# Linear-attention scan and two MLPs on one core: raw weights loaded into the tiles of their parts, prefix products spread by TensorE in the first block, a longer look ahead in the scheduler

## The chip, the core and the metric

The kernel runs on one core of a Trainium2 chip. The metric is the time of the core in microseconds (us), lower is better. The core has a matrix engine (PE), three other compute engines (DVE, ACT, POOL) that work from on-chip memory (SBUF; PE writes to PSUM, which DVE and ACT can read), and DMA queues. Here every transfer is issued by one queue, SP's, in the order of the program. Each engine executes its own instructions in the order written; across engines they wait for semaphores.

## What is computed

```python
def reference(x, a, B, C, moe_w_gate, moe_w_val, moe_w_out, moe_rms_g,
              moe2_w_in, moe2_w_out):          # weights arrive as float64
    # 1. scan over 24 chunks of 32 steps; batch 4, 8 heads, 768 steps, D 32, N 16
    la = log(clip(a, 1e-6, 1)); cum = cumsum(la, within the chunk)
    M  = (C B^T) * exp(cum_i - cum_j) * causal
    y  = M x + (C state) * exp(cum)
    state = exp(sum la) * state + sum_j B_j x_j exp(cum_end - cum_j)
    # 2. y becomes t[3072, 256]
    xn = t / sqrt(mean(t*t) + 1e-6) * moe_rms_g
    t  = (silu(xn @ w_gate) * (xn @ w_val)) @ w_out       # 256 -> 1536 -> 256
    # 3.
    h  = t @ w_in                                          # 256 -> 2048
    return (h * clip(h + 3, 0, 6) / 6) @ w_out2            # 2048 -> 256
```

## The kernel before

**Arithmetic.** A matmul in fp32 is done as three in fp32r: every operand is split into a high part (the value cast to fp32r) and a low part (the value minus the high part), and PE makes high·high, low·high and high·low (`mm3`, L642). Activations are split too: `xh`, `xl` are the parts of a block's input, `gh`, `gl` those of a hidden product.

**Weights.** They arrive as 8-byte floats and are turned into fp32 on the chip. For each tile f, `weights()` (L578 to L623) issues a load of the raw words (L585), then `low` and `high` on ACT (L598, L594), `join` and `sign` on DVE (L602, L607; integer operations on whole tiles), the high part as a cast on ACT or DVE (L245, L247) and the low part as a subtraction on DVE or POOL (L241, tiles `w1l`, `w2l`). There are 12 tiles of 128x768 for the first MLP (768 KB raw) and 16 of 128x512 for the second (512 KB raw). Raw tiles of the first go through a ring of six: three in the still unused result array `yT`, three (`rawx`) beside it. The intermediate fp32 tile has two places, also in `yT`. For the second MLP, `open2` frees the memory of the attention part and opens `w2h`, `w2l` and a ring of two raw tiles and two intermediate tiles (`cv`).

**Order of the work.** The 3072 rows fall into six blocks of 512. Each block needs four pieces of the scan (`attention(k)`, 24 in all), a norm, and then, in phase A, 12 steps: a step is 12 matmuls of 512 columns into `hps`, then on ACT a silu (L670), on DVE the product `p` (L678), `gh` on ACT (L685), `gl` on POOL or DVE (L241) and 6 matmuls into `acc`. The attention of the next block lies between the steps of a block. Phase B, the second MLP, has 16 steps per block (6 matmuls into `hps`, 6 into `acc`; L672 on ACT, L680 on DVE).

A piece k of attention: scores C·B on PE (L393); the decay matrix L as a scan on DVE (L366), which in the first block reads `aps`, a copy of the decays that PE spreads over the partitions (L358), and later a tile that a DMA spreads; the product SM on DVE (L402), two per piece; `bh` and `ch` on POOL or DVE (L241); the state step on PE (L411) and V on DVE (L422, L424); the result `y` on PE (L456, L462); its squares and transpose on ACT or DVE; the row mean on PE (L481) and `v` on DVE (L487). `ch` and V need P, the running products of the decays, spread over partitions: DVE makes them (`prefix`, L284), a DMA writes them to DRAM (`pref`, L298), and one DMA per piece reads them back spread (`ld_P`, L339). The norm ends with `rps` on PE (L532), the scaling on DVE (L538), `xh` on ACT and `xl` on DVE or POOL.

**The scheduler.** `Plan` holds all operations with estimated durations and dependences and simulates them: an engine that is free takes the ready operation with the longest tail (plus a boost). If an operation of much higher priority becomes ready within `WAIT` = 200 ns, the engine stays idle for it. Pieces of the first block have a boost of `BOOST0` = 15000. `either(n)` lets an operation go to DVE or POOL. In the first block's gaps PE multiplies zeros (`idle`, L305) as far as the first norm.

## Time and profile before

| | |
|---|---|
| runs, median (all) | 684.55 us (681.31, 684.55, 684.65) |
| profiled execution: its time, its span | 682.43 us, 680.3 us |
| PE busy | 659.6 us (97%) |
| DVE, ACT, POOL busy | 321.5, 292.3, 272.4 us |
| first matmul of the first MLP (first `hps`) | 39.69 us |
| norm of the second block (`rps`) | 99.20 us |
| norms of blocks three to six | 157.29, 219.35, 281.39, 342.53 us |
| last wait of PE that the trace shows | ends at 423.46 us |

All times of the trace count from the span's start. A block of phase A is the time from one `rps` to the next; phase B fills the time from 423.46 us to the end.

### The profile page before, as it was taken

What the parts mean: (1) busy time and instruction counts of PE and PEld (TensorE: products, weight loads), DVE (VectorE), ACT (ScalarE), POOL (GpSimd) and SP (SyncE); (2) the same over time, 40 slices, a digit from 0 to 9 for tenths busy, and PEclk for the clock granted to TensorE, in tenths of its full rate; (3) what the DMA queues carried; (4) which work ended last, traced back from release to release, by engine and by line L of the source; (5) the groups of instructions that cost most, each with busy time, mean ns of one, the idle gap of its engine ahead of it and who ended that gap; (6) DMA issues with size and microseconds to landing.
All of it is one profiled execution on the core that took longest, in us unless ns stands there. A gap on an engine that the chain in (4) does not pass through costs nothing.

```text
span 680.3 us, 10547 instructions
## 1 busy us (share of the span) xinstructions
PE 659.6 (97%) x4240; PEld 535.2 (79%) x4240; DVE 321.5 (47%) x532; ACT 292.3 (43%) x485; POOL 272.4 (40%) x223
## 2 busy tenths in 40 slices
PE   8879899999999999999999998999999999999997
PEld 7767677778778877877888876888888888888886
DVE  4798874554355345523268886232322322332222
ACT  2464442223222322332245666455444545454543
POOL 3334243233332342242234435454554545545443
PEclk9998899999999999999999999999999999999999
DMA  6965311130231031130003330000000000000000
GB/s 226 283 199 205 144 55 54 57 109 1 55 109 55 15 96 55 55 117 2 1 31 125 129 119 31 1 1 31 1 0 32 1 31 1 0 32 1 31 1 31
DMA packets 24464, 42.91 MB, mean 63 GB/s; under 512 B 2112, under 2 KB 15712, under 8 KB 24416
## 3 DMA queue, kind: packets, MB, share of 16 engines
q1 hardware_dynamic: 24416, 42.25, 19.0%
q8 instruction: 33, 0.54, 0.3%
q14 instruction: 15, 0.12, 0.1%
HBM read 38.90 MB, written 3.34 MB: 62 GB/s over the span
## 4 chain that ended last, share of the span: by engine, by line
PE 85%; DVE 9%; ACT 3%; issue 2%; DMA 0%; POOL 0%; SPq 0%; ACTq 0%; DVEq 0%; POOLq 0%
PE hps L642 46%; PE acc L642 30%; PE sps L462 2%; DVE p L678 2%; PE sps L456 1%; DVE SM L402 1%; PE sps L481 1%; ACT p L670 1%; DVE V L424 1%; DVE yT L607 1%; PE sps L393 1%; PE aps L358 1%; PE idle L305 1%; DVE yT L602 1%; PE rps L532 1%
## 5 line engine op out<-in xcount | busy, mean ns | idle before, releaser
L241 POOL TENSOR_TENSOR gl<-p,gh 128x512 fp32r<-128x512 f32 x158 | 209.1, 1324 | 267.0 <-ACT gh L685 254.4
L685 ACT CAST gh<-p 128x512 fp32r<-128x512 f32 x168 | 104.5, 622 | 126.7 <-PE acc L642 119.3
L680 DVE SCALAR_TENSOR_TENSOR p<-p,hps 128x512 f32<-128x512 f32 x96 | 65.9, 686 | 167.1 <-ACT p L672 167.0
L672 ACT ACTIVATE p<-hps,half 128x512 f32<-128x512 f32 x96 | 66.0, 687 | 79.3 <-POOL gl L241 77.6
L642 PE MATMUL hps<-xh,w1h 128*128 128x512 f32 x288 | 92.4, 402 | 0.1
L670 ACT ACTIVATE p<-hps 128x512 f32<-128x512 f32 x72 | 42.8, 595 | 113.4 <-PE hps L642 98.7
L678 DVE TENSOR_TENSOR p<-p,hps 128x512 f32<-128x512 f32 x72 | 49.2, 684 | 89.1 <-ACT p L670 88.3
L642 PE MATMUL hps<-xl,w1h 128*128 128x512 f32 x288 | 89.9, 393 | 0.5 <-DVE xl L241 0.4
L642 PE MATMUL hps<-xh,w1l 128*128 128x512 f32 x288 | 90.0, 394 | 0.0
L642 PE MATMUL acc<-gh,w2l 128*128 128x512 f32 x192 | 74.7, 389 | 0.0
L642 PE MATMUL acc<-gh,w2h 128*128 128x512 f32 x192 | 74.7, 389 | 0.0
L642 PE MATMUL acc<-gl,w2h 128*128 128x512 f32 x192 | 74.7, 389 | 0.0
L642 PEld LDWEIGHTS hps<-xl,w1h 128*128 128x128 f32 x288 | 54.6, 190 | 13.1 <-DVE xl L241 1.3
L642 PEld LDWEIGHTS hps<-xh,w1l 128*128 128x128 f32 x288 | 54.6, 190 | 11.9
L642 PE MATMUL hps<-xh,w2h 128*128 128x512 f32 x192 | 59.6, 392 | 2.5 <-DVE p L680 2.0
L642 PEld LDWEIGHTS hps<-xh,w1h 128*128 128x128 f32 x288 | 53.0, 191 | 10.5 <-ACT xh L245 0.6
L642 PE MATMUL acc<-gh,w1h 128*128 128x512 f32 x144 | 61.2, 425 | 0.0
L642 PE MATMUL hps<-xh,w2l 128*128 128x512 f32 x192 | 59.2, 389 | 0.0
L642 PE MATMUL hps<-xl,w2h 128*128 128x512 f32 x192 | 59.2, 389 | 0.0
L642 PE MATMUL acc<-gh,w1l 128*128 128x512 f32 x144 | 56.7, 394 | 0.0
L642 PE MATMUL acc<-gl,w1h 128*128 128x512 f32 x144 | 56.5, 393 | 0.0
L241 POOL TENSOR_TENSOR bh<-cb,L 128x256 f32<-128x256 f32 x22 | 14.6, 662 | 81.4 <-PE sps L411 64.5
(95 smaller groups left out, 836.9 us busy)
## 6 DMA issues: line engine op xcount, KB each, us to landing
cb<-comb SPq DMA_DIRECT2D x20, 576.0 KB
raw<-w SPq DMA_DIRECT2D x16, 512.0 KB
L<-azero SPq DMA_DIRECT2D x40, 128.0 KB
yT<-w SPq DMA_DIRECT2D x6, 768.0 KB
rawx<-w SPq DMA_DIRECT2D x6, 768.0 KB
out<-yT SPq DMA_DIRECT2D x12, 256.0 KB
P<-pref SPq DMA_DIRECT2D x24, 64.0 KB
cb<-comb SPq DMA_DIRECT2D x4, 320.0 KB
```

What stands on the lines that cost most here:

```text
L241: eng[e].tensor_tensor(out=out, in0=a, in1=b, op=op)
L305: pe.matmul(out=T["idle"][:, :128], lhsT=zero, rhs=zero, start=True, stop=True)
L358: pe.matmul(out=ps[64 * q:64 * q + 64, p * CH:(p + 1) * CH], rhs=az[:, q], lhsT=eye[:96, c:c + 1].to_broadcast([96, SC]), start=True, stop ...
L393: pe.matmul(out=bank2(ws[p // 2], "sps")[:, p % 2, c * SC:(c + 1) * SC], lhsT=cb[r, BN + c * 128:BN + (c + 1) * 128], rhs=cb[r, CT + c * S ...
L402: dve.tensor_tensor(out=T["SM", k][:, q], in0=T["w", ws[t]][:, :, 0:CH], op=ALU.mult, in1=T["L", k].rearrange("j (p c) i -> j p (c i)", c= ...
L462: pe.matmul(out=o[p][c], lhsT=cb[:, q:q + 64], rhs=SM[:, p, SC * c:SC * c + SC], start=False, stop=True, skip_group_check=True)
L642: pe.matmul(out=o, lhsT=a, rhs=c, start=first and i == 0, stop=last and i == len(seq) - 1)
L670: act.activation(out=p[:, :n], in_=T["w", hid][:, 0, :n], func=AF.Silu)
L672: act.activation(out=p[:, :n], in_=T["w", hid][:, 0, :n], func=AF.Relu, scale=1.0 / 6.0, bias=half)
L678: dve.tensor_tensor(out=p, in0=p, in1=h, op=ALU.mult)
L680: dve.scalar_tensor_tensor(out=p, in0=p, scalar=1.0, in1=h, op0=ALU.min, op1=ALU.mult)
L685: act.copy(out=t[:, :n], in_=T["p", i][:, :n])
```

## The change

There are three parts.

1. *Raw weights.* A raw tile is loaded into the memory in which its high and low part will stand later (`wt1`, `wt2`; a tile of twice the columns). Neither MLP has a ring of raw tiles any more. The high part overwrites the raw words once the intermediate tile is complete. The intermediate tile has eight places (instead of two) for the first MLP and four for the second.
2. *Prefix products.* In the first block (pieces 0 to 3) P comes from PE: POOL builds two selector tiles `rep` in the setup, `spread_p` multiplies them with `ac` (two matmuls of 128 columns), `copy_p` copies the result out of PSUM. The four DMAs of P that went with these pieces are gone. The later pieces read P by DMA as before.
3. *Scheduler.* An operation with a boost of at least `BOOST0` is waited for up to `FIRST` = 900 ns. The two DMAs to DRAM have a latency of 5000 ns in the plan. `prefix` has the highest priority.

```diff
-    WAIT, MARGIN = 200, 3000
+    WAIT, FIRST, MARGIN = 200, 900, 3000
...
-            soon = min((r for r, s in future[e] if r < t + self.WAIT and s not in done
+            soon = min((r for r, s in future[e] if s not in done
+                        and r < t + (self.FIRST if ops[s][4] >= BOOST0 else self.WAIT)
                         and -tail[s] - ops[s][4] < pri - self.MARGIN), default=None)
...
-    w1h = [cp.tile([128, 768], F32R, name=f"w1h{f}") for f in range(F1)]
-    w1l = [cp.tile([128, 768], F32R, name=f"w1l{f}") for f in range(F1)]
+    wt1, wt2 = {}, {}
+    wp1 = ctx.enter_context(tc.tile_pool(name="wp1", bufs=1))
+    for f in range(F1):
+        wt1[f] = wp1.tile([128, 1536], F32, tag=f"w{f}", name="raw")
...
+    rep = [ap1.tile([96, 4 * B, 2, N], F32, name=f"rep{q}") for q in range(2)]
...
-    rawx = [ap1.tile([128, 1536], F32, name=f"rawx{f}") for f in range(NRAW - 3)]
...
-              "sq": 1, "rn": 1, "x": 2, "p": 3, "gh": 3, "gl": 3, "raw": NRAW, "tmp": 2,
-              "raw2": 2, "cv": 2, "w": 3, "acc": 2})
+              "sq": 1, "rn": 1, "x": 2, "p": 3, "gh": 3, "gl": 3, "tmp": 8, "cv": 4, "w": 3, "acc": 2})
...
+        for q, t in enumerate(rep):
+            pool.memset(t, 0.0)
+            pool.affine_select(out=t[:, :, q], in_=t[:, :, q], pattern=[[1, 4 * B], [0, N]],
+                               compare_op=ALU.not_equal, fill=1.0, base=0, channel_multiplier=-1)
...
-             w=[("azero", 0)], boost=1e4)
-        P.op({"DVE": ds(256)}, prefix, r=[("az", 0)], w=[("ac", 0)], boost=1e4)
+             w=[("azero", 0)], boost=1e4, lat=5000)
+        P.op({"DVE": ds(256)}, prefix, r=[("az", 0)], w=[("ac", 0)], boost=1e9)
...
-        P.op(dma(65536), ld_P, r=[("pref", 0)], w=[("P", k)], boost=bst)
         if not first:
+            P.op(dma(65536), ld_P, r=[("pref", 0)], w=[("P", k)], boost=bst)
...
+        def spread_p(e):
+            for q in range(2):
+                pe.matmul(out=bank2(ws[0], "sps")[:, 0, 128:256], rhs=ac[:, q],
+                          lhsT=rep[q].rearrange("k a e n -> k (a e n)")[:, CH * k:CH * k + CH],
+                          start=q == 0, stop=q == 1, skip_group_check=True)
+
+        def copy_p(e):
+            T["P", k] = ap3.tile([128, CH], F32, tag="P", name="P")
+            copy(e, T["P", k], T["w", ws[0]][:, 0, 128:256])
...
         def load(e):
-            r = raw(f)
+            r = tiles[f][:, 0 if wide else cols:]
...
         def hi(e):
-            copy(e, wh[f], T[kt if wide else kr])
...
+            tiles[f] = pool().tile([128, 2, cols], F32R, tag=f"w{f}", name=f"w{tag}")
+            copy(e, tiles[f][:, 0], T[kt])
...
-        stage2.append(ctx.enter_context(tc.tile_pool(name="wp2", bufs=2)))
+        for f in range(F2):
+            wt2[f] = wp.tile([128, 1024], F32, tag=f"w{f}", name="raw2")
+        stage2.append(ctx.enter_context(tc.tile_pool(name="wp2", bufs=4)))
```

The lines of the changed kernel stand 1 to 26 higher: join and sign are L623 and L628, SM is L424, `v` is L508, the scan is L371, `two` is L242, the cast on DVE is L248, and the parts of a weight tile are both called `w`.

**DVE at the start, from the mean of piece 0 to the SM of piece 2.** Each row is an instruction of the queue with its output and inputs; `yT` in L602 and L607 is the intermediate weight tile. Before:

```order
L602 SCALAR_TENSOR_TENSOR yT<-yT 128x768
L487 TENSOR_SCALAR v_299<-sps 128x1
L607 SCALAR_TENSOR_TENSOR yT<-yT 128x768
L402 TENSOR_TENSOR SM<-sps,L 128x256 x2
L422 COPY V_324<-sps 128x64
L424 SCALAR_TENSOR_TENSOR V<-V_324,P,sps 128x64
L247 COPY xT<-sps 128x2x128
L241 TENSOR_TENSOR ch<-cb,P 128x64
L602 SCALAR_TENSOR_TENSOR yT<-yT 128x768
L487 TENSOR_SCALAR v_299<-sps 128x1
L607 SCALAR_TENSOR_TENSOR yT<-yT 128x768
L402 TENSOR_TENSOR SM<-sps,L 128x256 x2
```

After, from the scan of piece 2 to the last SM of piece 2:

```order
L371 SCALAR_TENSOR_TENSOR L<-aps,eye_107 128x512
L508 TENSOR_SCALAR v_272<-sps 128x1
L424 TENSOR_TENSOR SM<-sps,L 128x256 x2
L444 COPY V_299<-sps 128x64
L371 SCALAR_TENSOR_TENSOR L<-aps,eye_107 128x512
L508 TENSOR_SCALAR v_272<-sps 128x1
L424 TENSOR_TENSOR SM<-sps,L 128x256 x2
L444 COPY V_360<-sps 128x64
L446 SCALAR_TENSOR_TENSOR V<-V_299,P,sps 128x64
L446 SCALAR_TENSOR_TENSOR V<-V_360,P,sps 128x64
```

The joins and signs of the first two weight tiles, which stood ahead of the SM of pieces 1 and 2, are gone from here; only attention is left.

**DVE between the SM of piece 5 and that of piece 6** (`w1l`, `w` are weight parts, `p` the products of the steps, `ch` one of attention). Before:

```order
L424 SCALAR_TENSOR_TENSOR V1_711<-V_339,P_501,sps_676 128x64
L424 SCALAR_TENSOR_TENSOR V_715<-V1_711,P_501,sps_676 128x64
L241 TENSOR_TENSOR w1l6_92<-yT_73,w1h6_80 128x768
L241 TENSOR_TENSOR ch_744<-cb_631,P_671 128x128
L602 SCALAR_TENSOR_TENSOR yT_73<-yT_73 128x768
L607 SCALAR_TENSOR_TENSOR yT_73<-yT_73 128x768
L487 TENSOR_SCALAR v0_633<-sps_676 128x1
L247 CAST w1h7_81<-yT_73 128x768
L366 SCALAR_TENSOR_TENSOR L_746<-L_746,eye8_114 128x512
L602 SCALAR_TENSOR_TENSOR yT_73<-yT_73 128x768
L678 TENSOR_TENSOR p_776<-p_776,hps_756 128x512
L607 SCALAR_TENSOR_TENSOR yT_73<-yT_73 128x768
```

After:

```order
L628 SCALAR_TENSOR_TENSOR yT_73<-raw_82,yT_73 128x768
L623 SCALAR_TENSOR_TENSOR yT_73<-yT_73,raw_83 128x768
L248 COPY xT_585<-sps_650 128x2x128
L242 TENSOR_TENSOR ch_734<-cb_611,P_624 128x128
L628 SCALAR_TENSOR_TENSOR yT_73<-raw_83,yT_73 128x768
L248 CAST w_741<-yT_73 128x768
L508 TENSOR_SCALAR v0_602<-sps_650 128x1
L623 SCALAR_TENSOR_TENSOR yT_73<-yT_73,raw_84 128x768
L628 SCALAR_TENSOR_TENSOR yT_73<-raw_84,yT_73 128x768
L248 CAST w_765<-yT_73 128x768
L704 TENSOR_TENSOR p_762<-p_762,hps_743 128x512
L623 SCALAR_TENSOR_TENSOR yT_73<-yT_73,raw_85 128x768
```

More joins and signs stand here than before, and no low part. From the SM of piece 5 to that of piece 7 DVE has 13 joins and signs where it had 8, and no low part where it had 4; POOL has 5 to 7 low parts where it had one.

**POOL in the same stretch.** Before:

```order
L241 TENSOR_TENSOR gl_673<-p_648,gh_661 128x512
L241 TENSOR_TENSOR bh_708<-cb_631,L_616 128x256
L241 TENSOR_TENSOR gl_735<-p_669,gh_713 128x512
L241 TENSOR_TENSOR w1l7_93<-yT_73,w1h7_81 128x768
L241 TENSOR_TENSOR gl_800<-p_776,gh_796 128x512
L241 TENSOR_TENSOR bh_832<-cb_751,L_746 128x256
L241 TENSOR_TENSOR gl_859<-p_798,gh_837 128x512
```

After:

```order
L242 TENSOR_TENSOR gl_684<-p_645,gh_674 128x512
L242 TENSOR_TENSOR bh_701<-cb_611,L_592 128x256
L242 TENSOR_TENSOR w_722<-yT_73,w_722 128x768
L242 TENSOR_TENSOR w_741<-yT_73,w_741 128x768
L242 TENSOR_TENSOR w_765<-yT_73,w_765 128x768
L242 TENSOR_TENSOR gl_794<-p_762,gh_787 128x512
L242 TENSOR_TENSOR w_816<-yT_73,w_816 128x768
L242 TENSOR_TENSOR gl_858<-p_790,gh_827 128x512
L242 TENSOR_TENSOR w_860<-yT_73,w_860 128x768
```

Where single low parts stood between the `gl`, three now stand in a row (`w_722`, `w_741`, `w_765`, tiles 5 to 7), and two more alternate with `gl`.

**DVE at the end of phase A.** `raw_3818` to `raw_3911` of before and `raw_3339` to `raw_3341` of after are the last raw tiles of the second MLP; L680 and L706 are the products of phase B. Before:

```order
L602 SCALAR_TENSOR_TENSOR cv<-cv,raw_3818 128x512
L678 TENSOR_TENSOR p<-p,hps 128x512
L607 SCALAR_TENSOR_TENSOR cv<-raw_3818,cv 128x512
L680 SCALAR_TENSOR_TENSOR p<-p,hps 128x512
L602 SCALAR_TENSOR_TENSOR cv<-cv,raw_3865 128x512
L607 SCALAR_TENSOR_TENSOR cv<-raw_3865,cv 128x512
L680 SCALAR_TENSOR_TENSOR p<-p,hps 128x512
L241 TENSOR_TENSOR gl<-p,gh 128x512
L602 SCALAR_TENSOR_TENSOR cv<-cv,raw_3911 128x512
L680 SCALAR_TENSOR_TENSOR p<-p,hps 128x512
L607 SCALAR_TENSOR_TENSOR cv<-raw_3911,cv 128x512
L241 TENSOR_TENSOR gl<-p,gh 128x512
```

After:

```order
L623 SCALAR_TENSOR_TENSOR cv<-cv,raw_3339 128x512
L242 TENSOR_TENSOR w_3727<-cv,w_3727 128x512
L628 SCALAR_TENSOR_TENSOR cv<-raw_3339,cv 128x512
L704 TENSOR_TENSOR p<-p,hps 128x512
L623 SCALAR_TENSOR_TENSOR cv<-cv,raw_3340 128x512
L628 SCALAR_TENSOR_TENSOR cv<-raw_3340,cv 128x512
L242 TENSOR_TENSOR gl<-p,gh 128x512
L623 SCALAR_TENSOR_TENSOR cv<-cv,raw_3341 128x512
L704 TENSOR_TENSOR p<-p,hps 128x512
L628 SCALAR_TENSOR_TENSOR cv<-raw_3341,cv 128x512
L242 TENSOR_TENSOR gl<-p,gh 128x512
L704 TENSOR_TENSOR p<-p,hps 128x512 x2
```

Before, the last conversions lie between the products of phase B; now all of them lie ahead of the first one.

## Rows read from the trace of the kernel before

**Rows 1.** The page: busy time of PE over the span, and the shares of the chain that ended last, by engine.

```profile
PE 659.6 (97%) x4240; PEld 535.2 (79%) x4240; DVE 321.5 (47%) x532; ACT 292.3 (43%) x485; POOL 272.4 (40%) x223
...
PE 85%; DVE 9%; ACT 3%; issue 2%; DMA 0%; POOL 0%; SPq 0%; ACTq 0%; DVEq 0%; POOLq 0%
```

**Rows 2.** Windows of the span: start and end, length in us, then busy us (and instructions) of PE, of its weight loads, of DVE, ACT and POOL, the granted clock of PE as a share of full speed, the share of the DMA engines and GB/s. The first is from the first `hps` to the norm of block 2; the second lies inside it, from the SM of piece 5 to that of piece 7; then a whole block, the last block of phase A with the change of phase, and phase B.

```profile
39.60:99.10 59.50, 51.52 (x424) 39.82 (x424) 48.43 (x74) 30.59 (x48) 22.81 (x18) 0.91 0.42 148
59.97:88.25 28.28, 24.62 (x210) 18.92 (x208) 24.83 (x34) 15.13 (x24) 9.21 (x8) 0.94 0.43 150
157.20:219.20 62.00, 61.72 (x498) 49.25 (x497) 29.58 (x57) 18.49 (x35) 19.94 (x17) 1.00 0.19 60
342.40:423.40 81.00, 78.55 (x345) 63.35 (x343) 64.61 (x83) 48.63 (x86) 33.29 (x23) 1.00 0.26 91
423.40:676.00 252.60, 252.54 (x1114) 209.13 (x1115) 74.43 (x108) 125.69 (x196) 124.81 (x97) 1.00 0.03 11
```

**Rows 3.** The same view for the tile `hps` alone: the number behind PE's time is that of the 512-column matmuls.

```profile
39.60:99.10 59.50, 29.13 (x108) 21.59 (x108) 5.97 (x9) 5.37 (x9) 0.91 0.42 148
157.20:219.20 62.00, 34.33 (x144) 26.74 (x144) 8.19 (x13) 7.17 (x12) 1.00 0.19 60
342.40:423.40 81.00, 52.97 (x216) 40.08 (x216) 13.06 (x20) 12.08 (x20) 1.00 0.26 91
```

**Rows 4.** The same for the tile `acc`.

```profile
39.60:99.10 59.50, 12.27 (x42) 8.11 (x42) 0.00 (x0) 0.00 (x0) 0.91 0.42 148
157.20:219.20 62.00, 19.39 (x73) 12.82 (x72) 0.68 (x1) 0.58 (x1) 1.00 0.19 60
342.40:423.40 81.00, 30.46 (x121) 22.52 (x120) 0.68 (x1) 0.58 (x1) 1.00 0.26 91
```

**Rows 5.** The chain that ended last, in order of time: start, us, what.

```profile
157.29 0.89 PE rps L532 x8
158.18 5.48 PE hps L642 x24
...
219.35 0.89 PE rps L532 x8
...
342.53 0.89 PE rps L532 x8
```

**Rows 6.** Windows with a granted clock under full speed, columns as in rows 2.

```profile
48.40:54.90 6.50, 6.01 (x16) 4.94 (x17) 4.84 (x7) 1.24 (x3) 2.94 (x2) 0.51 0.96 333
75.20:78.70 3.50, 3.50 (x37) 2.88 (x38) 1.85 (x3) 0.65 (x2) 0.57 (x2) 0.51 0.48 141
```

**Rows 7.** DVE's timeline while the first four pieces run: start, us, line, operation, output and inputs, in brackets the idle time ahead.

```profile
10.96 1.22 DVE L366 TENSOR_TENSOR_SCAN L<-aps,eye 128x512 f32<-128x512 f32 x1 [1.50 <-PE aps L358]
...
14.76 0.28 DVE L424 SCALAR_TENSOR_TENSOR V<-V,P,sps 128x64 f32<-128x64 f32 x1
...
18.18 0.95 DVE L607 SCALAR_TENSOR_TENSOR yT<-yT 128x768 int32<-128x768 int32 x1
...
22.96 0.96 DVE L607 SCALAR_TENSOR_TENSOR yT<-yT 128x768 int32<-128x768 int32 x1
...
27.73 1.45 DVE L241 TENSOR_TENSOR bh<-cb,L 128x256 f32<-128x256 f32 x1
...
36.30 0.94 DVE L602 SCALAR_TENSOR_TENSOR yT<-yT,rawx 128x768 int32<-128x768 int32 x1
37.28 0.97 DVE L607 SCALAR_TENSOR_TENSOR yT<-rawx,yT 128x768 int32<-128x768 int32 x1
```

**Rows 8.** PE's timeline at the start: the last spreading of decays, the `y` step of piece 0, the mean of piece 3, the first matmul of the first MLP.

```profile
14.65 1.09 PE L358 MATMUL aps<-az,eye 96*64 96x128 f32 x16
15.68 0.34 PE L456 MATMUL sps<-ch,V 32*64 32x64 f32 x8
...
32.05 0.61 PE L481 MATMUL sps<-ones,sq 128*128 128x1 f32 x4 [0.65 <-ACT xT L245]
...
39.69 1.08 PE L642 MATMUL hps<-xh,w1h 128*128 128x512 f32 x2
```

**Rows 9.** DVE's timeline in the first block: casts, a scan, a low part and the SM of pieces 5 and 7.

```profile
51.58 0.56 DVE L247 CAST w1h<-yT 128x768 fp32r<-128x768 f32 x1
...
59.97 0.74 DVE L402 TENSOR_TENSOR SM<-sps,L 128x256 f32<-128x256 f32 x2
...
66.08 2.76 DVE L366 TENSOR_TENSOR_SCAN L<-L,eye 128x512 f32<-128x512 f32 x1 [0.24 <-DMA L<-azero]
...
71.19 1.54 DVE L247 CAST w1h<-yT 128x768 fp32r<-128x768 f32 x1
...
73.25 0.94 DVE L241 TENSOR_TENSOR w1l<-yT,w1h 128x768 fp32r<-128x768 f32 x1
...
88.25 0.74 DVE L402 TENSOR_TENSOR SM<-sps,L 128x256 f32<-128x256 f32 x2
```

**Rows 10.** POOL's timeline in the same stretch.

```profile
65.92 1.83 POOL L241 TENSOR_TENSOR w1l<-yT,w1h 128x768 fp32r<-128x768 f32 x1 [2.69 <-DVE w1h L247]
71.02 1.29 POOL L241 TENSOR_TENSOR gl<-p,gh 128x512 fp32r<-128x512 f32 x1 [3.26 <-ACT gh L685]
...
86.28 0.63 POOL L241 TENSOR_TENSOR bh<-cb,L 128x256 f32<-128x256 f32 x1 [0.30 <-PE sps L411]
```

**Rows 11.** PE's timeline at the first steps of phase B.

```profile
423.46 0.73 PE L642 MATMUL hps<-xh,w2h 128*128 128x512 f32 x2 [1.41 <-DVE p L680]
```

50 lines of the change are left out of this document (26 added, 24 removed).

## The prediction

> **What bounds the kernel now.** I read the page first. PE is busy for 97% of the span and holds 85% of the chain that ended last; DVE holds 9% of it, the DMA queues nothing [rows 1]. An average over the span hides where the rest is, so I cut the span at the norms. In a whole block of phase A PE works 61.72 of 62.00 us, in phase B 252.54 of 252.60 [rows 2]: there nothing but fewer matmuls could help, and the change removes none. What can move is the start (until the first `hps` at 39.69 us [rows 8]), the first block, and the change of phase, where PE misses 2.45 of 81.00 us [rows 2].
>
> How much each loses is a matter of counting matmuls. Twelve `hps` steps at full clock make 24 matmuls in 5.48 us, so one costs 0.228 us [rows 5]. A whole block lasts 219.35 − 157.29 = 62.06 us [rows 5] and holds 144 `hps` and 72 `acc` [rows 3, 4] (the window cuts one more `acc`): 49.2 us; 0.9 for `rps`; the other 12.0 are its attention. The first block until the norm of block 2 has 108 and 42 [rows 3, 4] and the same four pieces of attention: 150 × 0.228 + 12.0 = 46.2 us. It takes 59.5 [rows 2]. So 13.3 us are lost there. [...] DVE is busy for 48.43 of the 59.50 us [rows 2], and PE's attention steps wait for its SM and the steps for its `p`. In the change of phase 216 + 121 matmuls [rows 3, 4] and an `rps` make 77.7 us of 81.0; 3.3 are lost, 1.41 of them in the last wait for DVE's `p` [rows 11].
>
> **The start.** P of piece 0 no longer goes through two DMAs. V of piece 0 ran at 14.76, behind the scan of piece 2; now it stands behind the scan of piece 1, which began at 10.96 and took 1.22 [rows 7]. With `ch` and two small V steps between (about 0.7) the `y` step of piece 0 starts at about 13.3 instead of 15.68 [rows 8]: −2.3 us, and it passes the last spreading of decays, 1.09 us [rows 8], on the way. Then weight work leaves DVE's queue: an L607 of 0.95 ahead of the SM of piece 1, one of 0.96 ahead of that of piece 2, and a `bh` of 1.45 ahead of that of piece 3 that POOL now makes [rows 7]. Each was partly under PE's scores: I take 0.5, 0.8 and 0.9. The mean of piece 3 so comes at 32.05 − 4.5 = 27.6 [rows 8]. Behind it join and sign of one tile, 0.94 and 0.97 [rows 7], stood ahead of the scaling; now a join and a cast stand there: another −0.7. First `hps` at about 34.5: **−5.2 us** (bounds −3 and −6).
>
> The added work costs nothing here: two matmuls of 128 columns per piece and a copy on ACT stand where PE multiplied zeros and ACT waited; if the zeros did not cover them, four times about a third of a spreading of 1.09 us [rows 8] would be 1.5 us. The selector tiles are made while PE waits for its first data. The trace has no row for them; setting them aside at nothing is a choice, with 2.6 us as the upper bound, what two `gl` of POOL (1.29 each, of as many columns) take [rows 10].
>
> **The first block.** The start is earlier because the weights are later. Before, four of twelve tiles had been joined when the first `hps` began; now one is, and the other eleven are converted beside the steps. From the SM of piece 5 to that of piece 7 (28.28 us; DVE busy for 24.83, POOL 9.21 [rows 2]) DVE gets five joins or signs more (5 × 0.95 [rows 7]) and a `gl` (about 0.7, two thirds of a low part's 0.94), and gives four low parts to POOL (4 × 0.94 [rows 9]): +1.7 us for DVE by itself. POOL loses a `gl` (1.29) and gets four to six low parts of 1.83 [rows 10]: +6.0 to +9.7.
>
> On paper POOL has room for that. The trace says that the two don't run side by side. A cast on DVE took 0.56 alone, and 1.54 when it began at 71.19 beside a `gl` on POOL (71.02, 1.29 long); a scan took 1.22 alone [rows 7], and 2.76 when it began at 66.08 beside a low part on POOL that ended at 67.75 [rows 9, 10]. In both DVE's instruction ends where POOL's end plus its own time lie: 72.87 and 68.97 reckoned, 72.73 and 68.84 seen. SM and `p`, with an input in PSUM, aren't held up. So I add both engines' work on SBUF in one row: before, 8 joins and signs 7.6, 3 casts 1.7, 4 low parts 3.8, 2 scans 2.4 and a `ch` 0.3 on DVE; 4 `gl` 5.2, a low part 1.8, 2 `bh` 1.3 and a `ch` of about 0.5 on POOL: 24.6 of the 28.3 us. After: 24.6 + 1.7 + 6.0 to 9.7 = 32.3 to 36.0 us, and with the 3.7 that were free before, 36 to 40.
>
> [...]
>
> The SM of piece 5 comes some 3.6 us earlier than 59.97, at about 56.4 (the start's 5.2, less 1.6 for the join and low parts that now lie ahead of it); the SM of piece 7 then at 56.4 + 32.3 = 88.7 to 56.4 + 36 = 92.4, against 88.25 [rows 9]. Behind it the second kernel has fewer conversions left, two joins and a low part fewer (3.7 us), of which I count a third back. The norm of block 2 comes at 99.2 − 1 to 99.2 + 5, with +2.3 as my value. Against the start's −5.2 the first block gives back **+7.5 us** (bounds +2 and +11). How POOL and DVE take turns the trace shows in a few rows only; the sum takes every instruction as exclusive, which is the nearest to the two rows that do collide.
>
> **Later blocks** have the same order on PE: nothing, under PE's 61.72 of 62.00 us.
>
> **The change of phase.** All sixteen raw tiles of the second MLP have their own place, so none waits for a ring, and the last conversion stands ahead of the first product of phase B. The 3.3 us lost [rows 3 to 5, 11] can vanish. But no tile can be loaded before the last norm has read the attention's memory, some 4 us after the `rps` at 342.53 [rows 5], where the ring had its first two loaded in advance; ACT then stands before its first conversion with the silu of the next step behind it, and DVE's queue, 64.61 of 81.00 us busy before [rows 2], gets the same work in fewer steps. A delayed `p` costs PE 0 to 2.6 us. I take −3.3 + 1.6: **−1.7 us** (bounds −3.3 and +2).
>
> **Sum:** −5.2 + 7.5 − 1.7 = +0.6 us on the profiled execution's 682.43 us: 683.0. The median of the runs is 2.1 us above that execution, so on the median's scale it is 685.2; the runs shown lie between 681.3 and 684.7, and I forecast **684 us**, between the two.
>
> **The rivals.**
> *A: the start's gain stays.* If POOL's extra low parts fall mostly beside SM, `p` and DVE's waits for PE (DVE was idle for 3.5 of the 28.3 us, and SM and `p` are not held up), the collisions cost 2 instead of 7.5 us in the block: −5.2 + 2 − 1.7 = −4.9, and if one of the half-clock stretches goes too (1.7 to 3.2 us), −8: 675 to 679. For it: PE multiplies zeros for less time and its steps come earlier. Against it: three low parts in a row on POOL, 5.5 us, with DVE's joins beside them. It decides if the norm of block 2 comes before 96.
> [...]
> *C: nothing moves but the start and what it gives back.* First `hps` earlier, the norm of block 2 at 99 ± 1.5, and the change of phase as before because ACT's wait for the late raw tiles takes what the ring cost: 0 ± 1.5, 683 to 686.
>
> **How the numbers follow.** The forecast with C, which ends in the same place, 0.43; A 0.30; B 0.27. 0.5% of 684.55 is 3.4 us, about what a measurement can tell: faster is below 681.1, slower above 688.0. A and B lie wholly beyond these, the forecast within: 0.30, 0.43, 0.27. For 8 in 10 the range takes the larger part of A and B: 677 to 690; the likeliest case alone has 681.5 to 687.5.
>
> **What would show it.** Right: first `hps` near 34.5; between the SM of pieces 5 and 7 joins of 1.5 to 2.5 us beside POOL's low parts; the norm of block 2 between 98 and 103; no wait of PE for `p` after 403, but one between 347 and 390. Wrong: joins of 0.95 beside POOL's low parts; a first `hps` later than 37; a wait at the change of phase as long as before; later blocks that aren't 62 us long.

## The result, and the profile after

The change makes the kernel slower: 689.9 us (median of 11, 688.8 to 696.6) against 682.45 us (median of 11), a ratio of 1.013 with a 95% interval of 1.009 to 1.017 (the two medians alone give 1.011). The ratios leave out executions more than 1.5% above the fastest of their kernel: two of the four of b_spread, one of the twelve of a_combo_k, two of the twelve of a_combo_k2. The executions of the changed kernel have two lengths, 688.8 to 689.9 and 695.4 to 696.6 us. The first profile caught a longer one (span 694.3 us), a second one of the same kernel a shorter one (span 687.1 us, time 689.03 us). The second trace was taken to see what parts the two; a short execution was to show the third spreading of the decays at 1.09 us and the first `hps` at 37 to 39, and it does (below). The median belongs to the shorter kind, so I set that one against before. The kernel before has two of eleven executions above the rest as well (687.6 and 687.7, the others 680.9 to 684.7); no trace shows one of these.

The page of the shorter execution, as in [rows 1]:

```profile
PE 662.5 (96%) x4202; PEld 536.9 (78%) x4202; DVE 317.9 (46%) x527; ACT 295.3 (43%) x490; POOL 279.6 (41%) x231
...
PE 80%; DVE 12%; ACT 4%; issue 2%; DMA 1%; SPq 0%; ACTq 0%; DVEq 0%
```

PE's share is the same 97 to 96%, but the chain now has 12% DVE instead of 9%. The windows, as in [rows 2] (first `hps` to the norm of block 2, SM of piece 5 to SM of piece 7, a whole block, the change of phase):

```profile
37.60:104.30 66.70, 54.70 (x427) 42.03 (x426) 54.36 (x76) 35.02 (x53) 35.70 (x23) 0.85 0.38 138
61.30:93.35 32.05, 25.61 (x204) 18.94 (x202) 29.98 (x36) 15.90 (x24) 20.57 (x13) 0.84 0.19 61
162.40:224.50 62.10, 61.82 (x499) 49.33 (x498) 27.36 (x57) 18.59 (x35) 20.16 (x17) 1.00 0.20 60
347.60:428.00 80.40, 76.92 (x336) 61.66 (x335) 57.66 (x78) 51.52 (x89) 27.29 (x20) 1.00 0.27 105
```

The whole block is what it was, 62.1 us with PE at work for 61.82. The first block grew from 59.5 to 66.7 us, and its granted clock fell from 0.91 to 0.85. In the change of phase PE misses 3.48 us of 80.40, where it missed 2.45 of 81.00; the window after ends nine `acc` matmuls earlier in the work (112 for 121), so its idle time can be compared with before, its length can't. PE's matmuls that start the two spans, first in the longer execution (third spreading of decays, mean of piece 3, first `hps`; in the shorter one also the scores of pieces 2 and 3; the rows of before are [rows 8]):

```profile
13.49 1.98 PE L363 MATMUL aps<-az,eye 96*64 96x128 f32 x16
...
37.38 1.02 PE L502 MATMUL sps<-ones,sq 128*128 128x1 f32 x4 [0.33 <-ACT xT L246]
...
44.99 1.21 PE L667 MATMUL hps<-xh,w 128*128 128x512 f32 x4
```

and in the shorter one:

```profile
12.51 1.09 PE L363 MATMUL aps<-az,eye 96*64 96x128 f32 x16 [0.33 <-DVE L L371]
...
20.00 0.67 PE L415 MATMUL sps<-cb 32*128 32x64 f32 x16
...
24.57 1.13 PE L415 MATMUL sps<-cb 32*128 32x64 f32 x16
...
29.97 1.02 PE L502 MATMUL sps<-ones,sq 128*128 128x1 f32 x4 [0.34 <-ACT xT L246]
...
37.65 1.18 PE L667 MATMUL hps<-xh,w 128*128 128x512 f32 x4
```

The same instruction, a spreading of 16 matmuls, takes 1.98 us in one and 1.09 us in the other. I read the longer time as a lower clock of PE. The profile's granted clock does not say so; in the longer execution it reads 1.00 from 10 to 40 us, as in this window:

```profile
10.00:15.00 5.00, 5.00 (x50) 4.28 (x52) 1.79 (x5) 0.27 (x1) 0.98 (x2) 1.00 0.53 217
```

What speaks for the reading are instructions where the granted clock does read about half: before, at 0.51 from 75.2 to 78.7 us [rows 6], a `y` step (L462) takes 1.12 us at 75.64, against 0.69 at 61.66, and in the shorter execution, at 0.50 from 46 to 50 us (a window further below), a mean takes 1.01 us at 48.30, against 0.61 at 24.03. The longer execution shows such times all through its start (0.85 to 1.02 us for the means, 1.13 and 1.14 for the scores, 1.98 for every spreading). So I take it that PE is at the lower clock there from the first matmul to the zeros before the first `hps` (26 of them take 3.07 us from 42.17 on, where ten took 2.48 from 38.26 on). In the shorter execution it goes up by the third spreading (1.09 us), and by these times it is down again from the scores of piece 3 (1.13 us at 24.57, against 0.67 at 20.00) to the mean of piece 3 (1.02 us).

From here on a table serves, read from each kernel's timeline. Names that begin with a_ stand for the changed kernel with an edit, those with b_ for the kernel before with an edit. The columns: duration of the third spreading, start of the first `hps`, time from there to the `rps` of block 2, mean granted clock in that time, and time from the `rps` of block 6 to the span's end, all in us. (The time between the two `rps` is 243.3 to 243.5 in all of them but a_combo, 245.1.) A profile is one execution; the times are of all. Profiles of one order of the work differ too: the engines of a_w2ring have the order of the changed kernel as far as 100 us, and its block took 68.6 us, against 66.5 and 66.4.

```
kernel         3rd aps  first hps  block  clock  rps6-end   span    times: median (lowest to highest)
before           1.09     39.69    59.4   0.91    337.9    680.3    682.45 (680.9 to 687.7)
changed, short   1.09     37.65    66.5   0.85    339.5    687.1    689.9  (688.8 to 696.6)
changed, long    1.98     44.99    66.4   0.85    339.6    694.3
a_zeros          1.09     40.33    64.3   0.92    339.5    687.5    690.5  (689.4 to 693.0)
a_early          1.09     37.74    68.0   0.87    339.6    688.6    690.6  (689.9 to 692.1)
a_first200       1.98     46.42    62.1   0.92    339.7    691.7    693.4  (686.5 to 693.6)
a_lo_dve         1.98     45.22    60.5   0.92    340.0    689.1    690.8  (689.2 to 691.1)
a_w2ring         1.09     37.75    68.6   0.85    338.2    688.0    692.8  (689.9 to 695.7)
a_combo          1.09     38.28    60.8   0.92    338.2    682.4    682.9  (681.3 to 684.6)
a_combo_k        1.09     38.19    60.7   0.92    338.2    680.5    682.4  (680.4 to 691.2)
a_combo_k2       1.98     46.70    57.5   0.94    338.5    686.1    680.45 (677.6 to 692.7)
b_fewzeros       1.98     46.32    58.7   0.91    337.9    686.3    687.9  (687.4 to 688.5)
b_zeros          1.09     46.94    57.3   0.94    337.9    685.4    687.6  (684.8 to 688.3)
b_spread         1.09     36.98    57.3   0.97    338.2    675.9    682.8  (677.3 to 689.4)
b_spread_z       1.09     42.61    58.9   0.91    338.2    683.0    684.45 (679.2 to 686.9)
b_spread_s       1.98     47.54    60.8   0.89    338.2    689.9    691.4  (690.0 to 691.8)
b_spread_k       1.09     40.43    60.4   0.89    338.2    682.4    683.9  (680.3 to 686.4)
```

Against before the shorter execution reads: start −2.0, first block +7.1, change of phase +1.6, the rest +0.1: +6.8 us. The longer one: +5.3, +7.1, +1.7: +14.0 us.

### The profile page after: what moved, and what is told of

The parts are those of the page before. It is cut to its first block, busy times and chain, and to the rows that moved or that the text cites. A ratio compares the mean times of both kernels' runs of the same rounds, so it can differ in the third digit from the quotient of the medians.

```text
span 694.3 us, 10495 instructions
## 1 busy us (share of the span) xinstructions
PE 670.3 (97%) x4202; PEld 543.7 (78%) x4202; DVE 317.9 (46%) x527; ACT 295.4 (43%) x490; POOL 279.7 (40%) x231
## 3 DMA queue, kind: packets, MB, share of 16 engines
HBM read 38.63 MB, written 3.34 MB: 60 GB/s over the span
## 4 chain that ended last, share of the span: by engine, by line
PE 81%; DVE 12%; ACT 4%; issue 2%; DMA 1%; SPq 0%; ACTq 0%; DVEq 0%
PE hps L667 42%; PE acc L667 29%; PE sps L483 2%; DVE p L704 2%; PE sps L477 2%; PE sps L502 2%; DVE SM L424 1%; DVE cv L628 1%; ACT p L696 1%; DVE yT L623 1%; PE sps L415 1%; PE aps L363 1%; DVE yT L628 1%; DVE cv L623 1%; DVE V L446 1%
## 5 line engine op out<-in xcount | busy, mean ns | idle before, releaser
L242 POOL TENSOR_TENSOR gl<-p,gh 128x512 fp32r<-128x512 f32 x159 | 209.1, 1316 | 274.2 <-ACT gh L711 252.8
L667 PE MATMUL hps<-xh,w 128*128 128x512 f32 x960 | 263.4, 396 | 3.5 <-DVE p L704 3.5
L667 PEld LDWEIGHTS hps<-xh,w 128*128 128x128 f32 x960 | 180.3, 190 | 42.8 <-DVE p L704 6.3
L667 PE MATMUL acc<-gh,w 128*128 128x512 f32 x672 | 212.3, 397 | 0.0
L667 PE MATMUL hps<-xl,w 128*128 128x512 f32 x480 | 149.5, 393 | 0.0
L706 DVE SCALAR_TENSOR_TENSOR p<-p,hps 128x512 f32<-128x512 f32 x96 | 65.9, 687 | 176.3 <-ACT p L698 176.2
L667 PEld LDWEIGHTS acc<-gh,w 128*128 128x128 f32 x672 | 123.3, 188 | 26.4
L667 PE MATMUL acc<-gl,w 128*128 128x512 f32 x336 | 131.5, 392 | 1.6 <-POOL gl L242 1.6
L667 PEld LDWEIGHTS hps<-xl,w 128*128 128x128 f32 x480 | 91.0, 190 | 20.1 <-DVE xl L242 0.4
L698 ACT ACTIVATE p<-hps,half 128x512 f32<-128x512 f32 x96 | 66.4, 691 | 83.1 <-POOL gl L242 82.2
L667 PEld LDWEIGHTS acc<-gl,w 128*128 128x128 f32 x336 | 63.3, 188 | 15.7 <-POOL gl L242 2.0
L242 POOL TENSOR_TENSOR bh<-cb,L 128x256 f32<-128x256 f32 x24 | 16.2, 677 | 84.4 <-PE sps L433 65.7
L371 DVE TENSOR_TENSOR_SCAN L<-L,eye 128x512 f32<-128x512 f32 x20 | 31.6, 1579 | 27.0 <-DMA L<-azero 27.0
L242 POOL TENSOR_TENSOR w<-yT,w 128x768 fp32r<-128x768 f32 x10 | 21.2, 2121 | 19.9 <-ACT w L246 8.8
L424 DVE TENSOR_TENSOR SM<-sps,L 128x256 f32<-128x256 f32 x48 | 18.3, 416 | 7.8 <-PE sps L415 7.2
```

The lines of the kernel that those rows point to most:

```text
L242: eng[e].tensor_tensor(out=out, in0=a, in1=b, op=op)
L371: dve.tensor_tensor_scan(out=L, data0=T["aps", k] if first else L, data1=flat(eye8), initial=0.0, op0=ALU.mult, op1=ALU.add)
L424: dve.tensor_tensor(out=T["SM", k][:, q], in0=T["w", ws[t]][:, :, 0:CH], op=ALU.mult, in1=T["L", k].rearrange("j (p c) i -> j p (c i)", c= ...
L667: pe.matmul(out=o, lhsT=a, rhs=c, start=first and i == 0, stop=last and i == len(seq) - 1)
L698: act.activation(out=p[:, :n], in_=T["w", hid][:, 0, :n], func=AF.Relu, scale=1.0 / 6.0, bias=half)
L706: dve.scalar_tensor_tensor(out=p, in0=p, scalar=1.0, in1=h, op0=ALU.min, op1=ALU.mult)
```

## The experiments

### Zeros more or fewer: the start

The start was the largest miss, 7 to 10 us from what was forecast. The theory, called Z: PE multiplies fewer zeros (29 instead of 56 up to the first `hps`), and whether its clock goes up early hangs on that. First, more zeros in the changed kernel (a_zeros), fewer in the kernel before (b_fewzeros), no other edit:

```diff
# a_zeros, in the changed kernel
-    SLACK, BIAS = 400, 600
+    SLACK, BIAS = 100, 600
-                    t += ns if t > cold else 2 * ns
+                    t += ns if t > cold else 450
-            P.fill = idle, 225, 1200, 6000, len(P.ops)
+            P.fill = idle, 130, 1200, 6000, len(P.ops)
# b_fewzeros, in the kernel before
-    SLACK, BIAS = 400, 600
+    SLACK, BIAS = 900, 600
```

> The changed kernel with more multiplications of zeros at the start (70 in place of 29; the kernel before has 56), nothing else moved. Theory Z (the start is late because PE, with fewer zeros to multiply, works at the lower level of its clock: a spreading of decays took 1.98 us throughout in the changed kernel, 1.09 us from the third on in the kernel before): the third spreading takes 1.1 us, the first hps comes at 34 to 37 us instead of 44.99, and the time falls by 3 to 9 us against the changed kernel's 689.9. Rival S (the products spread by PE, their copy and the selector tiles make the start long): spreadings may get shorter, the first hps stays at 43 us or later, the time stays at 689 or gets worse by the zeros.

> The kernel before with fewer zeros at the start (30 in place of 56), nothing else changed. Theory Z: its spreadings, scores and means take the longer times too (1.98, 1.13 and 1.01 us in place of 1.09, 0.67 and 0.61), the first hps comes 4 to 8 us later than 39.69, the time rises by 4 to 8 us. Rival S: zeros only fill gaps; the first hps stays within 1 us of 39.69 and the time within 1 us of the kernel before.

PE's timeline of b_fewzeros, the third spreading and the first `hps`:

```profile
12.14 1.98 PE L358 MATMUL aps<-az,eye 96*64 96x128 f32 x16
...
46.32 0.83 PE L642 MATMUL hps<-xh,w1h 128*128 128x512 f32 x2
```

With fewer zeros alone the kernel before shows the longer spreadings to the last, its first `hps` comes 6.6 us later and the time rises to 687.9 us (ratio 1.0095, 1.0076 to 1.0113): theory Z, and its size. No other part of the change is in that kernel. In a_zeros the spreadings take 1.09 us again, and the first `hps` comes at 40.33, behind the zeros that now stand in front of it rather than behind its inputs. The block fell with it by only 2 us; the time stayed (690.5 us), so that the first `hps` at 34 to 37 and the gain of 3 to 9 us did not come. So fewer zeros explain the longer executions, and more zeros do not take back the loss of the shorter ones.

Then the zeros of the first 12 us alone:

```diff
# a_early, in the changed kernel
-                while t + ns + self.SLACK < s:
+                while t + (130 + 100 if t < 12000 else ns + self.SLACK) < s:
                     out.append((t, -1, fn, None))
-                    t += ns if t > cold else 2 * ns
+                    t += 450 if t < cold else 130 if t < 12000 else ns
```

> The changed kernel with more zeros in the first 12 us of the plan alone (the later gaps as in the changed kernel). Theory Z: clock up from the second spreading on, first hps at 37 to 40.3 us (the zeros ahead of the first hps cost a part of the gain when they were denser everywhere), the block up to the norm of block 2 64 to 66 us, as DVE and POOL set it, time 686 to 690. Rival: the block is long because PE's clock falls in it after a cold start; then it comes down to 60 to 62 with the earlier start, time 681 to 685.

First `hps` at 37.74 as in the shorter execution, and the four times within 2.2 us of one another (689.9 to 692.1): the longer kind did not occur in these four. The block was 68.0 us, more than the 64 to 66 expected: the rival, that the block is long because the start was cold (spreadings of 1.98 us to the last), falls.

### The prefix products by themselves

```diff
# b_spread, in the kernel before: rep, spread_p, copy_p and prefix's priority as in
# the change; no ld_P in the first block; nothing else
-        P.op(dma(65536), ld_P, r=[("pref", 0)], w=[("P", k)], boost=bst)
         if not first:
+            P.op(dma(65536), ld_P, r=[("pref", 0)], w=[("P", k)], boost=bst)
```

> The kernel before with the prefix products of the first block by PE (part 2 of the change) and nothing of parts 1 and 3. Its zeros at the start fall with it (two in place of four between the first two spreadings, none in place of three behind the second). Theory Z: as few zeros as in the changed kernel leave PE at the lower clock, spreadings take 1.98 us to the last, first hps at 43 to 47 us; from there on the kernel before: 59 to 60 us to the norm of block 2, 581 from that to the end; time 685 to 689. Rival (the late start belongs to the look ahead or to the raw tiles): first hps at 36 to 39.7, time 678 to 682.

Each came true within 0.7 us, in turn. Four executions took 677.3, 677.7, 687.9 and 689.4 us. The profile is a short one (third spreading, first `hps`):

```profile
12.78 1.09 PE L363 MATMUL aps<-az,eye 96*64 96x128 f32 x16
...
36.98 0.71 PE L663 MATMUL hps<-xh,w1h 128*128 128x512 f32 x2
```

The first `hps` comes 2.7 us earlier than before, and the block is 57.3 us at a mean clock of 0.97. Against the 683.3 us of before, run beside it, part 2 of the change alone (with the priority of `prefix`) is worth 6 us in two executions and costs 5 to 6 in the other two. That the clock makes the difference here is inferred from the two profiles of the changed kernel and from b_spread_s; the two longer executions of b_spread have no trace. Three tries to make the clock go up each time, and a control:

```diff
# b_spread_z: b_spread with the zeros of a_early
# b_spread_s: b_spread with two zeros more, ahead of the first spreading
-                while t + ns + self.SLACK < s:
+                while t + (250 if t < 4600 else ns + self.SLACK) < s:
                     out.append((t, -1, fn, None))
-                    t += ns if t > cold else 2 * ns
+                    t += 480 if t < cold else ns
# b_spread_k: b_spread with zeros in all gaps up to 31 us of the plan
+                while True:
+                    step, slack = ((450, 175) if t < cold else (300, 100) if t < 9500 else
+                                   (150, 80) if t < 31000 else (ns, self.SLACK))
+                    if t + min(step, ns) + slack >= s:
+                        break
+                    out.append((t, -1, fn, None))
+                    t += step
# b_zeros: the kernel before with the zeros of a_early
```

> The kernel before with PE's prefix products and with denser zeros in the first 12 us of the plan (the executions of the same kernel without them gave 677.3 and 677.7 us, and 687.9 and 689.4). If the long executions are those in which PE's clock stays at its lower level until the first hps, denser zeros leave only the short ones: every run between 676 and 681 us, third spreading of 1.09 us, first hps at 36 to 39. Rival (the two lengths have another cause, such as the transfers): both lengths remain, 676 to 681 and 687 to 690.

> The same with two more zeros only, ahead of the scores and ahead of the first spreading, where PE waits for its first data. If a little more work ahead of the second spreading is enough to lift the clock, every run lies between 675 and 680 us, up to 2 us below the kernel with denser zeros, since fewer zeros stand in the way. Rival (zeros before 6 us don't count for the clock at 11 us): two lengths as without them, 677 and 688.

> The kernel before with the denser zeros of the first 12 us and nothing else: the control for the two kernels with spread products. Its first spreadings are later by up to 1 us, its clock is up as it was; first hps at 39.5 to 41, time 681 to 684, no gain. If the gain of the others were the zeros' own, it would show here as 677 to 680.

> The kernel before with PE's prefix products and with zeros spread over the whole start up to the norm, as many per gap as in the kernel before or more (three between the first two spreadings instead of six). Theory Z: the clock rises by the third spreading in every execution and stays up to the first hps, which comes at 36.5 to 39; time 677 to 680, faster than the kernel before by 0.5 to 1%, without executions at 684 or more. Rival (more zeros delay the pieces by as much as the clock gives): first hps at 40 or later, or falls of the clock remain, 682 to 688.

All four missed; in b_spread_k the rival came true. Two zeros ahead of the first spreading did not lift the clock (b_spread_s: spreadings of 1.98 us in the profile, all four executions at 690.0 to 691.8 us). The denser zeros lifted it (third spreadings of 1.09 us in b_spread_z and b_spread_k), and cost what they gave. The control b_zeros shows how, by its mean of piece 0 and its first `hps`:

```profile
21.49 0.61 PE L481 MATMUL sps<-ones,sq 128*128 128x1 f32 x4 [0.33 <-ACT xT L245]
...
46.94 0.71 PE L642 MATMUL hps<-xh,w1h 128*128 128x512 f32 x2
```

The mean of piece 0, at 17.38 us before, waits until 21.49: eight, eight and ten zeros stood between the spreadings, the first eight at the lower speed (3.78 us, against 2.05 for the second eight). In b_zeros and b_spread_z the clock then fell once more ahead of the norm (the mean of piece 3 took 1.01 and 1.02 us). With zeros all along (b_spread_k) it stayed up (a mean of piece 3 of 0.60 us), but the first `hps` came at 40.43 and the time was that of before (ratio 1.0013, 0.9993 to 1.0033). How few zeros would lift it each time is left open.

### Low parts on DVE: the first block

```diff
# a_lo_dve, in the changed kernel
-        P.op(either(cols), lo, r=[kt, kh], w=[kl])
+        P.op(either(cols) if tag else {"DVE": d1(cols)}, lo, r=[kt, kh], w=[kl])
```

> The changed kernel with all low parts of the first MLP's weights made on DVE (0.95 us each) and none on POOL (1.83 each), which the scheduler otherwise chose for ten of twelve. [...] Rival (DVE's own queue is what is too long): DVE gets 9.5 us more, the stretch grows to 69 to 75 us, time 692 to 698.

The stretch from the first `hps` to the norm of block 2, in a_zeros and in a_lo_dve (columns as in [rows 2]):

```profile
40.30:104.90 64.60, 51.56 (x428) 40.03 (x427) 54.76 (x74) 33.11 (x50) 35.15 (x22) 0.92 0.39 135
```

```profile
45.20:105.80 60.60, 50.75 (x426) 39.73 (x424) 53.56 (x82) 33.89 (x51) 18.53 (x17) 0.92 0.40 132
```

POOL's busy time is halved (18.53 us for 35.15), DVE's is no longer (53.56 for 54.76) though it makes the low parts too: as I read it, what it works more it had lost in instructions stretched beside POOL's (a sign that takes 0.95 us by itself took 2.48 beside a low part, see below). The block went from 66.4 to 60.5 us, inside the 58 to 62 that I had expected if the two engines hold each other up; the rival wanted 69 or more. The two rows also set this apart from the clock: both have a mean clock of 0.92, and differ by 4.0 us; a_zeros and the changed kernel differ in the clock (0.92 and 0.85), and by 2.1 us, which is no more than a_w2ring and the changed kernel differ by at the same clock. The time, 690.8 us where 682 to 686 was expected, hides the gain, because the profiled execution was slow at the start (third spreading 1.98 us, first `hps` 45.22); the other three lie within 1.8 us of it and have no trace.

```diff
# a_first200, in the changed kernel
-    WAIT, FIRST, MARGIN = 200, 900, 3000
+    WAIT, FIRST, MARGIN = 200, 200, 3000
```

> The changed kernel with the look ahead for the first block set back from 900 to 200 ns; direct raw tiles and PE's prefix products stay. Two or three weight tiles are converted ahead of the first hps again, as before the change. Theory: the look ahead is what moves the weight conversions behind the first hps; without it the first hps comes no earlier than in the changed kernel (44 to 47 us, clock as there), but the first block loses 3 to 6 us of its 66.6, time 684 to 688. Rival (the conversions' place makes no difference, the low parts on POOL do): block within 1 us of 66.6, time within 2 us of 689.9.

The block is 4.3 us shorter (62.1), as expected. The time is not the 684 to 688 expected: three executions took 693.4 to 693.6 us and one 686.45, two lengths again, and the profile is of one of the three.

### The raw tiles of the second MLP: the change of phase

```diff
# a_w2ring, in the changed kernel
-            r = tiles[f][:, 0 if wide else cols:]
+            r = (stage2[1].tile([128, 1024], F32, tag="raw2", bufs=2, name="raw2") if tag
+                 else tiles[f][:, 0 if wide else cols:])
...
-              "sq": 1, "rn": 1, "x": 2, "p": 3, "gh": 3, "gl": 3, "tmp": 8, "cv": 4, "w": 3, "acc": 2})
+              "sq": 1, "rn": 1, "x": 2, "p": 3, "gh": 3, "gl": 3, "tmp": 8, "raw2": 2, "cv": 2, "w": 3, "acc": 2})
...
-        stage2.append(ctx.enter_context(tc.tile_pool(name="wp2", bufs=4)))
+        stage2.append(ctx.enter_context(tc.tile_pool(name="wp2", bufs=2)))
```

> The changed kernel with the raw tiles of the second MLP in a ring of two again, and two intermediate tiles, as before the change; nothing else. Theory (loading into the place of the parts is what costs 1.6 us at the change of phase, since the loads wait for the attention's memory and the conversions then come packed): from the norm of block 2 to the end 581.1 us as before in place of 582.7, ACT's wait of 3.39 us for the first raw tile gone, everything ahead of it as in the changed kernel. Rival (the later cost comes from elsewhere): 582.7 stays.

PE's waits from the last norm on, by what they were for (total, count, longest), before, in the changed kernel and in a_w2ring, and ACT's first conversion in the changed kernel:

```profile
PE hps L642 <- DVE p L680: 2.0, 3, 1.4
PE hps L642 <- DVE p L678: 0.5, 2, 0.3
```

```profile
PE hps L667 <- DVE p L704: 3.5, 6, 1.3
```

```profile
PE hps L668 <- DVE p L707: 2.0, 3, 1.4
PE hps L668 <- DVE p L705: 0.5, 2, 0.3
```

```profile
355.45 0.66 ACT L615 ACTIVATE cv<-raw 128x512 f32<-128x512 f32 x1 [3.34 <-DMA raw<-w]
```

From the `rps` of block 6 to the end it is 338.2 us with the ring and 339.5 to 340.0 in all six profiles without it (two of the changed kernel, a_zeros, a_early, a_lo_dve, a_first200). The place of the raw tiles, with the number of intermediate tiles that goes with it (four instead of two; the run sets both back), costs 1.3 us and more; the rest of the 1.6 lies within what the ring kernels differ among themselves (337.9 to 338.5). (From the norm of block 2 to the end it is 581.6, where I expected 581.1.) The time of this kernel, 692.8 us, has both lengths in it.

### The repairs together

a_combo joins a_early, a_lo_dve and a_w2ring; a_combo_k has the zeros of b_spread_k instead of a_early's; a_combo_k2 also sets the look ahead back to 200.

> Three repairs on the changed kernel together: the zeros of the first 12 us, all low parts of the first MLP's weights on DVE, the ring of two for the second MLP. If the three losses are separate and add: first hps at 37 to 40, 59 to 61 us to the norm of block 2, 581.1 to the end, 678 to 682, level with the kernel before or better. Rival (they share a cause, the start alone): no better than the zeros alone, 686 or more.

> The changed kernel with the same spread of zeros, all low parts of the first MLP's weights on DVE, and the ring of two for the second MLP. Clock up to the first hps at 37 to 39.5; block 60 to 61 us if the low parts on POOL cost what a_lo_dve gave back (6 us) whatever the clock at the start; from the norm of block 6 to the end 338.0. Time 680 to 683. If the block's loss belonged to a cold start, it would fall under 59, time under 680.

> As the kernel with the three repairs and the spread zeros, and with the look ahead back at 200 ns, so that two or three weight tiles are converted ahead of the first hps: first hps later by 1 to 1.5 us than with 900, the block shorter by 2 to 4 us; time 677 to 681. If the place of the conversions makes no difference once DVE and POOL don't block each other, the block stays and the time is that of the kernel with 900 plus 1.

The repairs add: block 60.8 in place of 66.4, end 338.2, time level with before, at the upper end of what was expected (a_combo 682.9 for 678 to 682, a_combo_k 682.4 for 680 to 683; ratios: a_combo 0.9998, 0.9985 to 1.0010; a_combo_k 0.9992, 0.9972 to 1.0013). With the look ahead at 200 the block is 57.5, shorter than before (59.4), and the median of all twelve is 680.45 us against 682.62. The ratio is 0.9962 (0.9940 to 0.9983); the means of all executions are 682.0 and 683.1, and it is not shown to be faster. The one profile is of the execution of 688 us, slow at the start (third spreading 1.98 us, first `hps` 46.70), so that neither the start of the ten shorter ones nor their block is shown.

## Why the prediction was wrong

**The sum.** Forecast +0.6 us on the profiled execution; measured +6.8 (shorter kind) and +14.0. The median lies at the upper edge of the range (677 to 690), but the likeliest case, within 0.5%, was the wrong one. Rival B, the slower one, with 0.27, had the side and the size (+6 to +8, 689 to 692 us) and its mark, the norm of block 2 after 103 us (104.1). No run shows the terms of its sum, a first block at +11 and in it 3.2 us for a third stretch at a lower granted clock; the profiles of the changed kernel show a block at +7.1 with two such stretches. The range took its upper part from that sum. Of the 6.2 us between +0.6 and +6.8 the start makes 3.2 and the change of phase 3.3; the first block, at +7.1 for +7.5, takes back 0.4. Two of the signs of being wrong came, a first `hps` later than 37 and waits at the change of phase as long as before; of the signs of being right, the long joins showed: joins and signs of 1.9 to 2.6 us beside POOL.

**The start, −5.2 forecast: −2.0, or +5.3.** The step that failed is "the added work costs nothing here", with the zeros named as its cover. They were taken as idle time that may be filled. The timeline of before showed more:

```profile
9.27 1.64 PE L358 MATMUL aps<-az,eye 96*64 96x128 f32 x16
...
12.23 1.09 PE L358 MATMUL aps<-az,eye 96*64 96x128 f32 x16
```

PE had sped up there (from 1.97 us for the first spreading to 1.09 for the third), with zeros between all spreadings. The changed order has 29 zeros for 56, which the order of PE's instructions shows ahead of any run, and none between the second spreading and the third. That fewer zeros are enough to keep PE slow up to the first `hps`, b_fewzeros shows: +6.6 us at the first `hps`, with no other edit. The added work itself is not what cost: b_spread has all of it, and in its profile the first `hps` came 2.7 us earlier than before. Five of the eleven executions of the changed kernel are of the longer kind. In the shorter kind the first piece's `y` step came earlier by 2.1 us (mean of piece 0 at 15.23 against 17.38), close to the 2.3 forecast. Of the 0.5 and 0.8 us for the weight work that left DVE's queue, 0.5 and 0.2 came (means of pieces 1 and 2 at 19.46 and 24.03, for 22.13 and 26.88). Then PE slowed down (scores of 1.13 us at 24.57, of 0.67 before), and the lead shrank: the mean of piece 3 came 2.1 us earlier, not 4.5. That more zeros would have saved this is not shown: in a_early PE stayed fast (a mean of piece 3 of 0.61 us), and the first `hps` came at 37.74 all the same. The tail behind the mean of piece 3 was 7.7 us, as before (7.6), not 0.7 shorter.

**The first block, +7.5 forecast: +7.1.** That DVE's instructions are stretched beside POOL's, on which this step rested, shows again (a sign of 2.48 us instead of 0.95); that the sum came out is in part luck. From the SM of piece 5 to that of piece 7 it was 32.05 us (28.28 before, [rows 2]), just under the forecast's 32.3 to 36; the +7.5 had some 7 us more in this stretch, and 3.8 came. From the first `hps` to the SM of piece 5 it was 23.65 us for 20.28, 3.4 more, where I had 1.6. Behind the SM of piece 7 I had counted 1.2 us back, and nothing came (10.8 us for 10.8). DVE's timeline of the shorter execution:

```profile
61.30 0.72 DVE L424 TENSOR_TENSOR SM<-sps,L 128x256 f32<-128x256 f32 x2
...
67.74 0.56 DVE L248 CAST w<-yT 128x768 fp32r<-128x768 f32 x1
...
68.28 0.95 DVE L623 SCALAR_TENSOR_TENSOR yT<-yT,raw 128x768 int32<-128x768 int32 x1
69.27 2.48 DVE L628 SCALAR_TENSOR_TENSOR yT<-raw,yT 128x768 int32<-128x768 int32 x1
...
72.86 2.26 DVE L623 SCALAR_TENSOR_TENSOR yT<-yT,raw 128x768 int32<-128x768 int32 x1
...
93.35 0.72 DVE L424 TENSOR_TENSOR SM<-sps,L 128x256 f32<-128x256 f32 x2
```

and POOL's low parts beside it:

```profile
68.38 2.55 POOL L242 TENSOR_TENSOR w<-yT,w 128x768 fp32r<-128x768 f32 x1 [1.69 <-DVE v L508]
72.48 1.82 POOL L242 TENSOR_TENSOR w<-yT,w 128x768 fp32r<-128x768 f32 x1 [1.55 <-ACT raw L619]
...
89.05 1.83 POOL L242 TENSOR_TENSOR w<-yT,w 128x768 fp32r<-128x768 f32 x1
```

A sign of 0.95 us took 2.48 where a low part of POOL ran beside it, a join 2.26: between the two SM five of 13 took 1.9 us or more. No wait of PE in the block is for a part of a weight: PE waited 7.0 us for `V` (6.2 before), 2.7 for `xT` and `sq` (1.1), 1.6 for a `gl` that stood behind a low part in POOL's queue, and 0.5 for `p`. What the sum had not counted is the clock, which I had only in rival B. Windows inside the block (columns as in [rows 2]):

```profile
42.00:46.00 4.00, 0.52 (x16) 0.52 (x16) 2.50 (x5) 3.61 (x6) 3.11 (x2) 0.88 0.00 0
46.00:50.00 4.00, 2.94 (x30) 2.54 (x23) 2.72 (x5) 1.81 (x4) 2.56 (x4) 0.50 0.61 188
50.00:54.00 4.00, 4.00 (x10) 3.05 (x10) 2.87 (x3) 1.30 (x2) 1.18 (x2) 0.50 0.73 261
74.00:78.00 4.00, 2.39 (x9) 1.41 (x6) 3.96 (x4) 1.74 (x4) 2.24 (x2) 0.72 0.00 0
78.00:82.00 4.00, 2.12 (x33) 1.45 (x32) 2.14 (x6) 2.54 (x5) 3.38 (x2) 0.50 0.00 0
82.00:86.00 4.00, 3.75 (x11) 3.18 (x12) 3.96 (x5) 1.00 (x2) 2.95 (x2) 0.50 0.69 215
```

PE works for 0.52 us of the four from 42 to 46, the rest being its wait of 3.48 us for DVE's `V`, and then stands at a granted clock of 0.50 for the next eight; the same from 76 to 86, behind the wait for `gl`. Before, there were two such stretches too, of 6.5 and 3.5 us [rows 6]; now each is about 10. Behind each of these two waits PE so lost time a second time; that the wait is what brought the clock down is my reading, and no run tests it. By the first windows after and in [rows 2], PE's busy time in the block grew by 3.2 us with the same work (54.70 for 51.52) and its idle time by 4.0 (12.00 for 7.98).

How the 7.1 us divide by cause is not shown. At an equal clock the low parts on POOL are worth 4.0 us (a_zeros against a_lo_dve), but each of two edits by itself gives back more: 5.9 us (a_lo_dve) and 4.3 (a_first200), together more than the whole, so the low parts on POOL and the conversions placed later overlap. What all profiles with the look ahead of 900 agree on is that the block is 60.5 to 60.8 us with the low parts on DVE (a_lo_dve, a_combo, a_combo_k) and 64.3 to 68.6 without (both of the changed kernel, a_zeros, a_early, a_w2ring).

**The change of phase, −1.7 forecast: +1.6.** The step that failed is the sign of the sum −3.3 + 1.6. ACT stood for 3.34 us before its first conversion, as foreseen, and the delayed `p` cost PE 1.26 us at 363.55; but the 3.3 did not vanish. PE waits for `p` six times between 363 and 409 instead of five times between 406 and 424, 3.5 us in place of 2.5:

```profile
363.55 1.20 PE L667 MATMUL hps<-xh,w 128*128 128x512 f32 x4 [1.26 <-DVE p L704]
...
399.06 1.20 PE L667 MATMUL hps<-xh,w 128*128 128x512 f32 x4 [1.13 <-DVE p L704]
```

With the ring back (a_w2ring) the waits are those of before. I counted the old waits as gone because their place was empty; that it is the sixteen conversions, squeezed into fewer steps, that make `p` late at the new place is argued from DVE's order, not shown.

**Later blocks** were right: 62.1 us, and 243.5 us between the norms of blocks 2 and 6, against 243.3.
